# First 256 tokens' queries and keys by f32 loads of SyncE and ScalarE with a cast on chip, in a fused attention and gated FFN kernel

## The chip, the cores and the metric

The kernel runs on one core of a Trainium2 chip. Its engines each work through a list of instructions of their own, in order: TensorE (PE: matrix products and transposes; PEld is its loading of weights), VectorE (DVE), ScalarE (ACT), GpSimd (POOL) and SyncE (SP). SyncE, ScalarE and GpSimd issue the DMAs, GpSimd those that change the type on the way. An instruction can wait on semaphores; everything behind it on its engine then waits too. The metric is the device time of one execution in microseconds (us), lower is better.

## The reference

```python
# q, k, v: (4, 8, 768, 64) f32; heads 0, 2, 6 are "retrieval" heads; n_sink 4, window 64
scores = q @ k.T / sqrt(64)
causal = rel >= 0                                   # rel = query position - key position
stream_keep = causal & (is_sink | (rel < window))
mask = causal for retrieval heads, stream_keep for the other five
a = softmax(where(mask, scores, -1e9)); attn = a @ v
x = attn, heads side by side                        # (3072, 512)
g, val = x @ w_gate, x @ w_val                      # (512, 1536) each
ffn_out = (gelu(g) * val) @ w_out                   # (1536, 512)
out = x + sigmoid(x @ w_res) * ffn_out              # f32
```

## The kernel before

All products are in f16 with f32 sums. The 3072 tokens go in six chunks of 512 (`CHUNKS`); chunk 0 is the first 512 tokens of batch 0, chunk 1 takes the last 256 of batch 0 and the first 256 of batch 1, and so on. Heads go in pairs (`PAIRS`: (0,2), (4,6), (1,3), (5,7)). For a chunk, attention makes the scores of a pair (`scores`, key on the partition), their exponentials on ScalarE, masks on DVE (`ea`, `eb`, `es` are these tiles; `ek` is for the four sink keys), the sums with the values (`weigh`; `va`, `vs`, `vk` are the values as loaded, shifted by some rows, and of the sinks), a normalization into `xtok` (f32) and `x` (f16), and the features-by-tokens form `xT`, by transposes on TensorE or, for the fourth pair of chunks 3, 4 and 5, by a transposing DMA of SyncE (`to_features_dma`, `xT<-x`). Then come the gate and value products (`xT,wg` and `xT,wv`), GELU and product (`hT`), the output products (`wo,hT`), the residual gate (`wr,xT`), and the products of a scheme in the manner of Strassen (`hS`, `wS`, `wt`). Chunk 0's attention runs in two halves of 256 tokens.

Queries and keys have to stand features-by-tokens (`qT`, `kT`). For chunks 0 and 1 `loads_rows` does it: GpSimd loads rows with a cast from f32 to f16 into a staging buffer (`qks`), TensorE transposes (`L682`, tile `ps`), and DVE or ScalarE evacuates (`L693`). In chunk 0 the first 256 tokens (y=0) come in four loads of four heads, k and q in turn, the next 256 (y=1) in two loads of eight heads. Later chunks use transposing DMAs of SyncE (`loads_natural`). `load_weights` and `values` make the loads of the weights and of v, on GpSimd.

Every piece of work is a task of a graph, numbered as it is built. Nothing decides the order at build time: two tables written out in the file do. `PLAN` is the list of the task numbers in the order of emission, a letter behind a number chooses the engine of a task that several can do (a ACT, d DVE, g and p POOL, s SP), and `w39` puts in 39 filler matmuls on the tile `blank`. `PLACES` gives the slot of each buffer. Each engine gets its tasks in the order of `PLAN`; waits follow from dependences and buffers. The fillers' results are not used:

```python
    for _ in range(180):
        warm = Buf(P_ps, "warm")
        G.add("pe", 0.11, lambda e, warm=warm: e.matmul(at(warm)[:, 0:256], lhsT=blank[:, 0:128], rhs=blank[:, :], start=True, stop=True),
              [t_blank], 1e9, bufs=[warm], name="warm")
```

Of the kernel before, what the change touches and what calls it, by code (L numbers as in the profile page):

```python
# [4 lines left out]
NHEAD = 8  # L5
# [425 lines left out]
def build_kernel(nc, q, k, v, w_gate, w_val, w_out, w_res, out):  # L431
# [153 lines left out]
    def values(b, a, z, base, each, on_engines=False):  # L585
# [43 lines left out]
        for lo in cuts:  # L629
            hi = lo + 1 if each else z  # L630
            ts = []
            for dst, src, off in ((0, 64, 1), (64, 0, 0)):
# [4 lines left out]
                ts[-1].late = 2.5  # L637
            for i in range(lo, hi):
                BB.vstok[i] = ts

    def loads_rows(c, si, b, a, z):

        BB = batch(b)
# [867 lines left out]
```

## Time and profile before

| | |
|---|---|
| runs | 265.31, 265.75, 266.03 us; median 265.75 |
| span of the profiled execution | 264.3 us; with the 1.45 us that the median has beside it, 265.75 |
| TensorE busy | 254.5 us (96%), 77 of 3421 matmuls are fillers |
| DVE, ScalarE, GpSimd busy | 210.8, 155.3, 106.8 us |
| first transposes of q and k | 8.16 us |
| first scores | 11.05 us |
| first gate or value product | 22.26 us |

A span is one execution on the profiler's clock. A row of the timeline gives start, duration, engine, line, operation, output tile and inputs; a row of a stretch gives the busy time of each engine in it. The chain of work that ended last is followed back from the last instruction, each step to what released it. A DMA's landing is counted from its issue.

### The profile page before, as it was taken

What the parts mean: (1) busy time and instruction counts of PE and PEld (TensorE: products, weight loads), DVE (VectorE), ACT (ScalarE), POOL (GpSimd) and SP (SyncE); (2) the same over time, 40 slices, a digit from 0 to 9 for tenths busy, and PEclk for the clock granted to TensorE, in tenths of its full rate; (3) what the DMA queues carried; (4) which work ended last, traced back from release to release, by engine and by line L of the source; (5) the groups of instructions that cost most, each with busy time, mean ns of one, the idle gap of its engine ahead of it and who ended that gap; (6) DMA issues with size and microseconds to landing.
All of it is one profiled execution on the core that took longest, in us unless ns stands there. A gap on an engine that the chain in (4) does not pass through costs nothing.

```text
span 264.3 us, 8077 instructions
## 1 busy us (share of the span) xinstructions
PE 254.5 (96%) x3421; PEld 180.7 (68%) x3421; DVE 210.8 (80%) x473; ACT 155.3 (59%) x274; POOL 106.8 (40%) x145
## 2 busy tenths in 40 slices
PE   8999999999999999999998899999999998999993
PEld 5657655558567578667677477579588677778891
DVE  1499555999988978678999677999687976877985
ACT  1277534964554998564883356884655995445511
POOL 8996741990000998013976620711500111110021
PEclk9999999999999999999999999999999999999998
DMA  7999999999297999968999994899589509050004
GB/s 69 166 139 178 207 196 191 188 158 115 82 271 99 141 123 135 182 154 182 136 97 124 152 138 93 200 123 104 69 92 237 101 2 122 7 77 2 2 2 159
DMA packets 102067, 33.17 MB, mean 125 GB/s; under 512 B 88720, under 2 KB 97168, under 8 KB 102032
## 3 DMA queue, kind: packets, MB, share of 16 engines
q0 software_dynamic: 74704, 18.88, 77.3%
q1 hardware_dynamic: 26896, 13.26, 25.0%
q8 instruction: 27, 0.44, 0.7%
q10 hardware_dynamic: 432, 0.52, 0.5%
q14 instruction: 8, 0.07, 0.1%
HBM read 29.36 MB, written 10.49 MB: 151 GB/s over the span
## 4 chain that ended last, share of the span: by engine, by line
PE 87%; DVE 8%; DMA 3%; issue 1%; ACT 0%; DVEq 0%
PE ps L477 45%; PE ps L478 30%; PE ps L850 4%; PE ps L1414 4%; DMA xT<-x 3%; PE ps L682 2%; PE ps L974 2%; PE ps L1063 1%; DVE xtok L1041 1%; DVE x L1039 1%; DVE vk L598 1%; PE ps L941 1%; DVE hS L1251 0%; DVE hT L1228 0%; DVE vs L617 0%
## 5 line engine op out<-in xcount | busy, mean ns | idle before, releaser
L539 POOL DMA_DIRECT2D qks<-in_q_dram x37 | 33.2, 983 | 48.3 <-DMA qT<-qks 26.1
L1359 POOL DMA_DIRECT2D out_dram<-otile x16 | 15.6, 975 | 76.8 <-DVE otile L1355 66.2
L477 PE MATMUL ps<-xT,wg 128*128 128x512 f16 (+1 forms) x172 | 38.7, 337 | 1.4 <-DMA xT<-x 1.0
L477 PE MATMUL ps<-xT,wv 128*128 128x512 f16 (+1 forms) x172 | 38.5, 337 | 0.0
L1129 ACT ACTIVATE gact<-ps 128x512 f16<-128x512 f32 x38 | 22.1, 596 | 27.0 <-PE ps L477 18.0
L1131 DVE SCALAR_TENSOR_TENSOR hT<-gact,ps 128x512 f16<-128x512 f16 x38 | 25.8, 683 | 13.7 <-ACT gact L1129 5.8
L539 POOL DMA_DIRECT2D qks<-in_k_dram x37 | 34.8, 977 | 1.4 <-POOLq L1493 0.8
L1203 DVE TENSOR_TENSOR ps<-ps,otile 128x256 f32<-128x256 f32 x60 | 24.0, 428 | 7.7 <-PE ps L477 3.7
L1221 ACT ACTIVATE gact<-ps 128x512 f16<-128x512 f32 x30 | 16.6, 596 | 15.7 <-PE ps L477 10.8
L539 POOL DMA_DIRECT2D va<-in_v_dram x24 | 23.7, 1017 | 3.8 <-DVE va L534 3.8
L477 PEld LDWEIGHTS ps<-xT,wg 128*128 128x128 f16 x172 | 16.2, 98 | 13.1 <-DMA xT<-x 1.5
L477 PEld LDWEIGHTS ps<-xT,wv 128*128 128x128 f16 x172 | 16.6, 98 | 11.4 <-issue 0.2
L866 ACT ACTIVATE ea<-ps 128x1024 f16<-128x1024 f32 (+2 forms) x24 | 22.0, 925 | 1.4 <-PE ps L850 1.3
L1228 DVE SCALAR_TENSOR_TENSOR hT<-gact,ps 128x512 f16<-128x512 f16 x30 | 19.3, 682 | 2.6 <-PE ps L478 1.2
L1299 ACT ACTIVATE srs<-ps 128x512 f32<-128x512 f32 x22 | 13.1, 599 | 12.2 <-PE ps L478 7.8
L477 PE MATMUL ps<-wo,hT 128*128 128x256 f16 (+1 forms) x114 | 18.3, 296 | 0.0
L478 PE MATMUL ps<-xT,wg 128*64 128x512 f16 (+1 forms) x144 | 17.6, 344 | 0.0
L478 PE MATMUL ps<-xT,wv 128*64 128x512 f16 (+1 forms) x144 | 17.6, 344 | 0.0
L1041 DVE TENSOR_TENSOR xtok<-ps,rcp 128x512 f32<-128x512 f32 (+1 forms) x28 | 16.8, 608 | 0.6
L1331 DVE TENSOR_TENSOR otile<-otile,ps 128x256 f32<-128x256 f32 x33 | 13.1, 412 | 3.7 <-PE ps L477 2.4
L850 PE MATMUL ps<-qT,kT 64*128 64x64 f16 (+4 forms) x391 | 15.9, 213 | 0.1
L478 PE MATMUL ps<-wo,hT 128*64 128x256 f16 x216 | 15.6, 273 | 0.4 <-DVE otile L1325 0.4
(175 smaller groups left out, 590.4 us busy)
## 6 DMA issues: line engine op xcount, KB each, us to landing
out_dram<-xtok SPq DMA_DIRECT2D x4, 1024.0 KB, 4.8
out_dram<-otile POOLq DMA_DIRECT2D x16, 256.0 KB, 4.5
va<-in_v_dram POOLq DMA_DIRECT2D x24, 128.0 KB, 5.6
qks<-in_k_dram POOLq DMA_DIRECT2D x32, 64.0 KB, 4.9
qks<-in_q_dram POOLq DMA_DIRECT2D x32, 64.0 KB, 5.0
wv<-in_moe_w_val_dram POOLq DMA_DIRECT2D x3, 512.0 KB, 13.2
wg<-in_moe_w_gate_dram POOLq DMA_DIRECT2D x3, 512.0 KB, 11.4
wo<-in_moe_w_out_dram POOLq DMA_DIRECT2D x4, 384.0 KB, 20.9
```

The costliest lines, as they stand in the source:

```text
L477: return e.matmul(o, lhsT=lhsT, rhs=rhs, **k)
L478: return [e.matmul(o[h:h + 64], lhsT=lhsT[:, h:h + 64], rhs=rhs, **k) for h in (0, 64)][-1]
L539: return G.add(eng, issue, lambda e: e.dma_start(out_ap(), in_ap), deps, prio, bufs=bufs, dma=cost, name=name, grp=grp)
L850: return [e.matmul(at(scr)[:, oo:oo + w], lhsT=side(BB, qb, low, 1)[half, k0:k0 + 128], rhs=side(BB, qb, low, 0)[half, qq:qq + w], start=T ...
L866: return e.activation(out=o, in_=i_, func=AF.Exp, scale=SM_SCALE)
L1041: t2 = G.add("dve", c_dve(2 * n * 64), lambda e: e.tensor_tensor(out=xview(), in0=avv(0, DHEAD), in1=scale(), op=ALU.mult), [t1] + xdeps, ...
L1129: ta = G.add("act", c_act(512), (lambda gb=gb, ga=ga, gw=gw: lambda e: e.activation(out=at(ga)[:, :], in_=at(gb)[:, gw], func=AF.Gelu))(), ...
L1131: th = G.add("dve", c_dve(512), (lambda vb=vb, ga=ga, f=f, vw=vw: lambda e: e.scalar_tensor_tensor(out=hv(f), in0=at(ga)[:, :], scalar=0.5 ...
L1203: return G.add("dve", c_dve(256), lambda e: e.tensor_tensor(out=at(ps)[:, o], in0=at(ps)[:, BL], in1=at(es)[:, 0:256], op=ALU.add), deps, ...
L1221: ta = G.add("act", c_act(512), (lambda x=x, ga=ga, both=both: lambda e: e.activation(out=two(at(ga)[:, :]), in_=both(x), func=AF.Gelu))() ...
L1228: th = G.add("dve", c_dve(512), (lambda x=x, f=f, ga=ga, both=both: lambda e: e.scalar_tensor_tensor(out=two(hv(f)), in0=two(at(ga)[:, :]) ...
L1359: t = G.add("pool", 1.0, (lambda ot=ot, r0=r0: lambda e: e.dma_start(out[r0:r0 + 128, :], at(ot)[:, :], accum_op=ALU.add))(), ends + [stor ...
```

## The change

A new function `loads_first` takes the queries and keys of tokens 0 to 255 of batch 0. It makes eight loads in f32, one for each pair of heads and each of k and q (128 KB each): k on SyncE, q on ScalarE. Each goes into a part of a staging buffer that is read as f32, is cast to f16 into one of the buffers that otherwise hold `x` (a task `c16`, on DVE, ScalarE or GpSimd), is transposed on TensorE (`L667`, two pairs of heads at a time) and evacuated (`L677`). `loads_rows` now makes only y=1 in chunk 0, k and q in one staging buffer. In the last chunk, the transposing DMAs of q and k of a token tile are one group (`grp`). `PLAN` and `PLACES` are new throughout: 35 fillers instead of 77, the first run of them 11 instead of 39; some copies go from DVE to ScalarE.

```diff
 PLAN = (
-    "1 0 14 214 16 210 211 212 215 2 5 w39 240 213 241d w2 228 216 229a w4 230 236 231d 217 237d w6 411 3 6 232 412 4 233d "
+    "0 222 220 224 218 214 212 5 216 1 225 223 16 17 210 2 235 3 234 6 215 236 217g 221a w11 232 233 219a 230 231 w3 431 "
...
+    def loads_first(b, a):
+        BB = batch(b)
+        lo = a * 128
+        qb, qo = qplace[b, a]
+        tok = {}
+        st, half = [Buf(P_st), Buf(P_st)], [Buf(P_x16), Buf(P_x16)]
+        view = lambda j, p: at(st[j])[:, :].bitcast(FP32)[:, p * 256:(p + 1) * 256]
+        h16 = lambda j, p: at(half[j]).rearrange("p c i k -> p (c i k)")[:, p * 256:(p + 1) * 256]
+        for p in ORDER:
+            h = PAIRS[p][0]
+            for j, src, eng in ((1, k, "sp"), (0, q, "act")):
+                ld = G.add(eng, 0.6, (lambda src=src, j=j, p=p, h=h: lambda e: e.dma_start(
+                    view(j, p).rearrange("p (x w) -> p x w", x=2),
+                    src[b, h:h + 3:2, lo:lo + 256, :].rearrange("x (p i) d -> p x (i d)", i=2)))(),
+                    [], -60, bufs=[st[j]], dma=0.5, name="ldf")
...
+                tok[j, p] = G.flex({e: (0.4, cast(e)) for e in ("dve", "act", "pool")}, [ld], -205, bufs=[st[j], half[j]], name="c16")
+        for k_ in (0, 2):
+            ps_ = sorted(ORDER[k_:k_ + 2])
+            for j in (1, 0):
+                scr = Buf(P_ps, "scr0")
+                to, o0 = (BB.kt, lo) if j else (qb, qo)
+                tt = G.add("pe", 0.3, (lambda scr=scr, j=j, ps_=ps_: lambda e: [
+                    e.transpose(out=at16(scr)[64 * x:64 * x + 64, (m * 2 + i) * 128:(m * 2 + i + 1) * 128],
+                                in_=h16(j, p)[:, x * 128 + i * 64:x * 128 + i * 64 + 64], identity=ident[:, :])
+                    for m, p in enumerate(ps_) for i in range(2) for x in range(2)])(),
+                    [t_ident] + [tok[j, p] for p in ps_], 40 * k_ - 205, bufs=[half[j], scr], name="qkT")
...
     def loads_rows(c, si, b, a, z):
-        st = [Buf(P_st), Buf(P_st)] if c == 0 else [Buf(P_st)] * 2
+        st = Buf(P_st)
...
-        for y in range((z - a) // 2):
+        first = 0 if c else 1
+        for y in range(first, (z - a) // 2):
             lo = (a + 2 * y) * 128
-            for gi, (h0, h1) in enumerate(((0, 4), (4, 8)) if c == 0 and y == 0 else ((0, 8),)):
-                for j, src in ((1, k), (0, q)):
...
+            if c == 0:
+                loads_first(b, a)
             (loads_rows if c < ROWS_UNTIL else loads_natural)(c, si, b, a, z)
```

Three places in the engines' lists. In the rows, `[waits ...]` are semaphores: `cnt_` of an engine's progress, `dma_` of one DMA; `x7` is a run of seven equal instructions. First, TensorE from its first instruction on; before:

```order
L1414 MATMUL ps<-blank 128x256 [waits cnt_dve]
L1414 MATMUL ps<-blank 128x256 x38
L682 MATMUL ps<-ident,qks 64x128 [waits cnt_pool,dma_214]
L682 MATMUL ps<-ident,qks 64x128 x7
L1414 MATMUL ps<-blank 128x256 x2
L682 MATMUL ps<-ident,qks 64x128 [waits dma_210]
L682 MATMUL ps<-ident,qks 64x128 x7
L1414 MATMUL ps<-blank 128x256 x4
```

and after:

```order
L1457 MATMUL ps<-blank 128x256 [waits cnt_dve]
L1457 MATMUL ps<-blank 128x256 x10
L667 MATMUL ps<-ident,x 64x128 [waits cnt_dve,cnt_act,cnt_pool]
L667 MATMUL ps<-ident,x 64x128 x7
L667 MATMUL ps<-ident,x 64x128 [waits cnt_dve,cnt_act]
L667 MATMUL ps<-ident,x 64x128 x7
L1457 MATMUL ps<-blank 128x256 x3
L893 MATMUL ps<-qT,kT 128x64 [waits cnt_dve]
```

The first transposes (of q, tile `x` holds the casted rows) now wait for DVE's and ScalarE's casts and GpSimd's identity instead of a DMA, and the first scores (`L893`, formerly `L850`) stand behind 16 transposes and 14 fillers instead of 32 and 51.

Second, ScalarE and DVE at the start. ScalarE before:

```order
L693 ACT_TABLE_LOAD
L693 ACTIVATE kT<-ps 128x2x256 [waits cnt_pe]
L866 ACTIVATE es<-ps 128x512 [waits cnt_pe]
L866 ACTIVATE ea<-ps 128x768 [waits cnt_pe]
L693 ACTIVATE qT<-ps 128x2x256 [waits cnt_pe]
```

and after:

```order
L652 DMA qks<-in_q_dram 128x2x128 x4
L658 ACT_TABLE_LOAD
L658 ACTIVATE x<-qks 128x256 [waits dma_220]
L658 ACTIVATE x<-qks 128x256 [waits dma_218]
L909 ACTIVATE es<-ps 128x512 [waits cnt_pe]
```

The four loads of q are issued ahead of the table load, and two casts (of q and of k of heads 1 and 3) come before the first exponential. DVE before:

```order
L532 MEMSET vk 128x520 [waits cnt_dve]
L534 MEMSET va 128x48
L693 COPY kT<-ps 128x2x256 [waits cnt_pe]
L693 COPY qT<-ps 128x2x256 [waits cnt_pe]
L693 COPY kT<-ps 128x2x256 [waits cnt_pe] x2
L693 COPY qT<-ps 128x2x256 [waits cnt_pe] x2
L902 TENSOR_TENSOR ea<-ea,m_causal 128x2x256 [waits cnt_pool,cnt_act]
```

and after:

```order
L659 CAST x<-qks 128x256 [waits dma_224]
L659 CAST x<-qks 128x256 [waits dma_222]
L534 MEMSET va 128x48 [waits cnt_dve]
L659 CAST x<-qks 128x256 [waits dma_214]
L677 COPY qT<-ps 128x2x256 [waits cnt_pe]
L677 COPY kT<-ps 128x2x256 [waits cnt_pe]
L659 CAST x<-qks 128x256 [waits dma_210]
L532 MEMSET vk 128x520
L659 CAST x<-qks 128x256 [waits dma_212]
L677 COPY qT<-ps 128x2x256 [waits cnt_pe]
L677 COPY kT<-ps 128x2x256
L532 MEMSET vk 128x520
```

Three casts stand ahead of DVE's first evacuation, two casts and both memsets of `vk` among and behind the evacuations of the first 256 tokens.

Third, TensorE in chunk 4, up to the first product that waits for the transposing DMA of the fourth pair; before (the DMA is `dma_1419`):

```order
L478 MATMUL ps<-vk,ek 64x65 x12
L478 MATMUL ps<-wt,hT 64x256 [waits cnt_dve]
L478 MATMUL ps<-wt,hT 64x256 x5
L478 MATMUL ps<-wo,hT 64x256 [waits cnt_dve]
L478 MATMUL ps<-wo,hT 64x256 x11
L478 MATMUL ps<-wt,hT 64x256 x6
L1063 MATMUL ps<-ident,x 64x128 [waits cnt_dve,cnt_act]
L1063 MATMUL ps<-ident,x 64x128 x15
L478 MATMUL ps<-wr,xT 64x512 [waits cnt_dve]
L478 MATMUL ps<-wr,xT 64x512 x7
L478 MATMUL ps<-xT,wv 64x512 [waits cnt_dve,cnt_act]
L478 MATMUL ps<-xT,wv 64x512 x7
```

(next comes the wait for `dma_1419`), and after, in two pieces that follow each other (the DMA is `dma_1431`):

```order
L478 MATMUL ps<-vk,ek 64x65 x6
L478 MATMUL ps<-wt,hS 64x256 x2
L478 MATMUL ps<-wt,wS 64x256 x4
L1106 MATMUL ps<-ident,x 64x128 [waits cnt_dve,cnt_act]
L1106 MATMUL ps<-ident,x 64x128 x15
L478 MATMUL ps<-wo,hS 64x256 [waits cnt_act]
L478 MATMUL ps<-wo,hS 64x256 x5
L478 MATMUL ps<-wo,hT 64x256 [waits cnt_act]
L478 MATMUL ps<-wo,hT 64x256 x11
```

```order
L478 MATMUL ps<-xT,wv 64x512 [waits cnt_act,cnt_dve]
L478 MATMUL ps<-xT,wv 64x512 x3
L478 MATMUL ps<-xT,wg 64x512 [waits cnt_dve]
L478 MATMUL ps<-xT,wg 64x512 x7
L478 MATMUL ps<-wo,hS 64x256 x2
L478 MATMUL ps<-wo,wS 64x256 x4
L478 MATMUL ps<-xT,wv 64x512 [waits cnt_dve]
L478 MATMUL ps<-xT,wv 64x512 x3
L478 MATMUL ps<-xT,wg 64x512 x4
L478 MATMUL ps<-xT,wg 64x512 [waits dma_1431]
```

The piece before has in front of it, further up, 56 sums with values (`va,ea`) and others between the sums of the fourth pair (12 `vk,ek`) and the wait; after the change no sum with `va,ea` is left between the last `vk,ek` and the wait: what stands there is what the two pieces show.

More of the change, by code (lines that the diff above doesn't have):

```diff
@@ L639, in values, with cast, ev, fn @@
                 BB.vstok[i] = ts
+    def loads_first(b, a):
[13 more added lines that the diff above has]
+                    [], -60, bufs=[st[j]], dma=0.5, name="ldf")
+                def cast(on, j=j, p=p):
+                    return lambda e: (e.activation(out=h16(j, p), in_=view(j, p), func=AF.Copy) if on == "act" else
+                                      e.tensor_copy(out=h16(j, p), in_=view(j, p)))
+                tok[j, p] = G.flex({e: (0.4, cast(e)) for e in ("dve", "act", "pool")}, [ld], -205, bufs=[st[j], half[j]], name="c16")
[9 more added lines that the diff above has]
+                    [t_ident] + [tok[j, p] for p in ps_], 40 * k_ - 205, bufs=[half[j], scr], name="qkT")
+                tt.mode = "col"
+                def ev(on, scr=scr, to=to, o0=o0, ps_=ps_):
+                    def fn(e):
+                        o = at(to)[:, ps_[0]:ps_[1] + 1:ps_[1] - ps_[0], o0:o0 + 256].rearrange("c m (p i) -> c m p i", i=2)
+                        i_ = at16(scr)[:, 0:512].rearrange("c (m i p) -> c m p i", m=2, i=2)
+                        return e.tensor_copy(out=o, in_=i_) if on == "dve" else e.activation(out=o, in_=i_, func=AF.Copy)
+                    return fn
+                t = G.flex({"dve": (c_dve(512), ev("dve")), "act": (c_act(512), ev("act"))}, [tt], 40 * k_ - 205,
+                           bufs=[scr, to], name="qkE")
+                for p in ps_:
+                    for i in range(a, a + 2):
+                        (BB.ktok if j else BB.qtok)[p, i] = t
@@ L647, in loads_rows, with sv, piece @@
         tok = {}
-        def sv(j, h0, h1, y):
-            if c == 0:
-                return at(st[j])[:, :].rearrange("p (h w) -> p h w", h=NHEAD)[:, h0:h1, y * 128:y * 128 + 128]
-            return at(st[j])[:, :].rearrange("p (j h w) -> p j h w", j=2, h=NHEAD)[:, j, h0:h1, :]
-        def piece(j, h, i, y):
-            o = h * 256 + y * 128 if c == 0 else (j * NHEAD + h) * 128
-            return at(st[j])[:, o + i * 64:o + (i + 1) * 64]
-        for y in range((z - a) // 2):
-            lo = (a + 2 * y) * 128
-            for gi, (h0, h1) in enumerate(((0, 4), (4, 8)) if c == 0 and y == 0 else ((0, 8),)):
-                for j, src in ((1, k), (0, q)):
-                    t = dma("pool", base + 4 * gi + 8 * y + 1 - j, (h1 - h0) * n * (0.092 if c else 0.089),
-                            (lambda j=j, h0=h0, h1=h1, y=y: lambda: sv(j, h0, h1, y))(),
-                            src[b, h0:h1, lo:lo + 256, :].rearrange("h (p j) d -> p h (j d)", j=n), bufs=[st[j]])
-                    t.late = 1.0 if c else 0.7
-                    for h in range(h0, h1):
-                        tok[j, h, y] = t
+        def sv(j):
+            return at(st)[:, :].rearrange("p (j h w) -> p j h w", j=2, h=NHEAD)[:, j]
+        def piece(j, h, i):
+            o = (j * NHEAD + h) * 128
+            return at(st)[:, o + i * 64:o + (i + 1) * 64]
+        first = 0 if c else 1
+        assert (z - a) // 2 - first == 1
+        for y in range(first, (z - a) // 2):
+            lo = (a + 2 * y) * 128
+            for j, src in ((1, k), (0, q)):
+                t = dma("pool", base + 8 * y + 1 - j, NHEAD * n * 0.092, (lambda j=j: lambda: sv(j))(),
+                        src[b, :, lo:lo + 256, :].rearrange("h (p j) d -> p h (j d)", j=n), bufs=[st])
+                t.late = 1.0
+                for h in range(NHEAD):
+                    tok[j, h, y] = t
         values(b, a, z, base + (10 if c == 0 else 2), False, c == 0)
         per = 2 if c == 0 else 4
-        for y in range((z - a) // 2):
+        for y in range(first, (z - a) // 2):
             lo = (a + 2 * y) * 128
@@ L679, in loads_rows, with tr @@
                     to = BB.kt if js[0] else qb
-                    def tr(e, items=items, scr=scr, y=y):
+                    def tr(e, items=items, scr=scr):
                         return [e.transpose(out=at16(scr)[64 * x:64 * x + 64, (m * n + i) * 128:(m * n + i + 1) * 128],
-                                            in_=piece(jj, h, i, y), identity=ident[:, :])
+                                            in_=piece(jj, h, i), identity=ident[:, :])
                                 for m, (p, jj) in enumerate(items) for i in range(n) for x, h in enumerate(PAIRS[p])]
                     tt = G.add("pe", c_mm(128, n) * len(items), tr, [t_ident] + [tok[jj, h, y] for p, jj in items for h in PAIRS[p]],
-                               pr, bufs=[st[js[0]], scr], name="qkT")
+                               pr, bufs=[st, scr], name="qkT")
                     tt.mode = "col"
@@ L726, in loads_natural @@
                 t = G.add("sp", 1.65, (lambda sv=sv, to=to, o0=o0: lambda e: e.dma_start(
-                    at(to)[:, :, o0:o0 + 128], sv(), transpose=True))(), ds, base, bufs=[st, to], dma=0.85, name="dT")
+                    at(to)[:, :, o0:o0 + 128], sv(), transpose=True))(), ds, base, bufs=[st, to], dma=0.85, name="dT",
+                          grp=("dT", b, i) if c == len(CHUNKS) - 1 else None)
                 t.late = 2.5
```

152 rows, old and new, of tables (PLACES, PLAN) are left out of this document.

## The prediction

> **What bounds the kernel now.** I read the page first: the busy times, the slices, the chain of work that ended last.
>
> ```profile
> span 264.3 us, 8077 instructions
> ...
> PE 254.5 (96%) x3421; PEld 180.7 (68%) x3421; DVE 210.8 (80%) x473; ACT 155.3 (59%) x274; POOL 106.8 (40%) x145
> ...
> PEclk9999999999999999999999999999999999999998
> ...
> PE 87%; DVE 8%; DMA 3%; issue 1%; ACT 0%; DVEq 0%
> ```
>
> TensorE is busy for 96% of the span and carries 87% of the chain. Some of that busy time is filler matmuls on a blank tile, so the question is in which stage TensorE is busy with nothing. Next came the table of stretches: start to first transposes, from there to the first gate/value matmul, the dense part after it (each row: stretch, length, busy time of PE, PEld, DVE, ACT, POOL with counts, granted clock, DMA share, GB/s).
>
> ```profile
> 0.00:8.16 8.16, 6.95 (x39) 5.08 (x40) 0.84 (x4) 1.28 (x1) 6.97 (x14) 1.00 0.93 87
> 8.16:22.26 14.10, 13.78 (x240) 8.99 (x240) 11.54 (x31) 8.68 (x19) 13.65 (x25) 1.00 1.54 152
> 22.26:139.00 116.74, 116.36 (x1268) 77.17 (x1268) 96.50 (x216) 76.99 (x131) 58.17 (x75) 1.00 1.37 158
> ```
>
> Until 8.16 us nothing useful runs on TensorE: its 39 matmuls are fillers. In the next 14.10 us DVE works 11.54 and 38 of TensorE's 240 matmuls are fillers. From 22.26 us on TensorE idles 0.38 us in 116.74: it is the bound there, so an earlier first gate/value matmul is worth its whole amount if nothing later takes it back. The timeline and the chain of the start say what holds that matmul (timeline: start, duration, engine, line, tile, count, idle before).
>
> ```profile
> 0.82 1.28 ACT L693 ACT_TABLE_LOAD   x1 [0.82 <-PEq L1493]
> ...
> 1.21 7.03 PE L1414 MATMUL ps<-blank 128*128 128x256 f16 x39 [1.21 <-DVE blank L511]
> ...
> 3.21 0.77 POOL L539 DMA_DIRECT2D qks<-in_q_dram  x1
> ...
> 8.16 0.41 PE L682 MATMUL ps<-ident,qks 128*64 128x128 f16 x8
> ...
> 8.62 0.69 DVE L693 COPY kT<-ps 128x512 f16<-128x512 f16 x1 [6.58 <-PE ps L682]
> ...
> 10.17 0.69 DVE L693 COPY qT<-ps 128x512 f16<-128x512 f16 x1 [0.87 <-PE ps L682]
> ...
> 11.72 0.69 DVE L693 COPY kT<-ps 128x512 f16<-128x512 f16 x1 [0.27 <-PE ps L682]
> ...
> 12.89 1.47 DVE L693 COPY qT<-ps 128x512 f16<-128x512 f16 x2 [0.47 <-PE ps L682]
> ...
> 22.26 1.03 PE L477 MATMUL ps<-xT,wv 128*128 128x256 f16 x8
> ```
>
> ```profile
> 14.28 0.41 DVE ea L902
> ...
> 23.10 0.44 DVE xtok L1041
> ```
>
> GpSimd issues the q load at 3.21 and TensorE's transposes follow at 8.16, 4.9 us later. From the first mask at 14.28 to a normalization at 23.10 the chain stands on DVE; before that DVE waits, up to 0.87 us, for TensorE's transposes, which wait for landings. So loads hold the first half of the stage, DVE the second.
>
> **The change, part by part.** Prices come from these rows: small hardware-queue DMAs, casts of twice the width, the `vk` memset, and last the landing of GpSimd's q and k loads in the first 8 us.
>
> ```profile
> L1371 SPq DMA_DIRECT2D out_dram<-otile x5: 332/578/1313, 72.7 to 260.3; - x5
> L1371 ACTq DMA_DIRECT2D out_dram<-otile x3: 338/338/375, 257.5 to 261.6; - x3
> ...
> DMA to landing us min/median/max: 1.7/2.0/3.7
> ```
>
> ```profile
> L1048 DVE CAST x<-xtok x2: 428/532/635, 141.8 to 219.9; 128x512 f16<-128x512 f32 x2
> ```
>
> ```profile
> L1047 ACT ACTIVATE x<-xtok x8: 621/629/632, 63.0 to 223.1; 128x512 f16<-128x512 f32 x8
> ```
>
> ```profile
> L532 DVE MEMSET vk<- x2: 492/492/492, 1.3 to 36.4; 128x520 f16 x2
> ```
>
> ```profile
> DMA to landing us min/median/max: 4.1/4.9/5.7
> ```
>
> (1) *The first transposes.* They need the identity, the first two q loads, a cast of one on ScalarE and of the other on DVE; the k pair behind them needs ScalarE's second cast. ScalarE starts at 0.82 and issues four loads (0.338 each by its own row, 0.578 by SyncE's: to 2.2 or 3.1), then the table load (1.28), which now stands behind the issues (to 3.5 or 4.4), then a cast of 256 elements, half the width of the row with 0.629, so 0.3 to 0.6: between 3.8 and 5.0, and I take the middle, 4.4. Landings are not the later branch by the nearest rows: stores of the same queues land in 1.7 to 2.0 us, so loads issued by 1.5 are there by 3.5. If they took what GpSimd's q took, 4.9, the transposes would start at 1.5 + 4.9 + 0.4 = 6.8. I take the stores, since the queue is the same: 8.16 − 4.4 = **−3.8 us** (from −4.4 to −1.4). Nothing hides it: eleven fillers end about 3.5 and TensorE then waits.
>
> (2) *DVE's new work.* DVE does five of the eight casts; three stand before its first evacuations, where it was idle, two among the evacuations: 2 × 0.27 to 0.43 (half the row's median up to its minimum), 0.7. One `vk` memset of 0.49 ran at 1.3 us in idle time, the other at 36.4; now both stand between evacuations: 1.0. **+1.7 us** (0.7 if waits for TensorE cover the memsets, 1.9 at most). Waiting behind them are the evacuations of the second pairs, then masks and ScalarE's exponentials.
>
> (3) *Idle on DVE closed.* From 8.62 to 14.28 before, DVE idled 0.87 + 0.27 + 0.47 = 1.6 us for transposes (the brackets of the timeline's rows). The y=1 loads are now issued second and third by GpSimd instead of after four others, so half of it should go: **−0.8** (0 to −1.6). The first gate/value matmul then stands at 22.26 − 3.8 + 1.7 − 0.8 = 19.4.
>
> (4) *GpSimd and the weights.* Four loads leave GpSimd's queue (4 × 0.8), one cast enters and waits for its landing, holding the later v and weight loads. The first gate weights move ahead of the first value weights. Weights have to be there at 19.4 and not 22.26: the first value and gate loads took
>
> ```profile
> DMA to landing us min/median/max: 5.9/13.2/16.8
> ...
> DMA to landing us min/median/max: 7.5/11.4/15.0
> ```
>
> (value, then gate). With gate issued near 9.9 and value near 13.9 (0.77 us an issue, by the q row, and about 0.5 a mask, copy or memset ahead of them), they land at 9.9 + 7.5 = 17.4 and 13.9 + 5.9 = 19.8. I cost it at 0; without that cover the value products wait up to about 0.5.
>
> (5) *Order of the rest.* Copies move from DVE to ScalarE (80% against 59% busy): 0, hidden behind TensorE. What can show is the feature DMA of chunks 3 to 5, `xT<-x` (its landing over all three; then chunk 4's alone; then the chain at chunk 3's and the timeline at chunk 4's).
>
> ```profile
> DMA to landing us min/median/max: 3.7/4.9/7.4
> ```
>
> ```profile
> L1054 SPq DMA_TRANSPOSE xT<-x x1: 1232/1232/1232, 180.8 to 180.8; - x1
> ...
> DMA to landing us min/median/max: 4.9/4.9/4.9
> ```
>
> ```profile
> 142.46 7.36 DMA xT<-x
> ...
> 149.86 2.33 PE ps L477 x10
> ```
>
> ```profile
> 179.30 0.38 PE L478 MATMUL ps<-vk,ek 128*64 128x65 f16 x12
> ...
> 183.80 0.82 PE L478 MATMUL ps<-wo,hT 128*64 128x256 f16 x12
> 184.45 0.50 PE L478 MATMUL ps<-wt,hT 128*64 128x256 f16 x6
> 184.78 0.62 PE L1063 MATMUL ps<-ident,x 128*64 128x128 f16 x16
> 185.23 1.03 PE L478 MATMUL ps<-wr,xT 128*64 128x512 f16 x8
> 186.09 1.47 PE L478 MATMUL ps<-xT,wv 128*64 128x512 f16 x12
> ```
>
> From starts, a 256-column half matmul costs 0.65/12 = 54 ns, a 512-column one 0.86/8 = 107 ns, 16 transposes 0.45. Chunk 4 before: the last sums of its fourth pair end at 179.68, the DMA is issued at 180.8 and lands at 185.7, 6.0 us after; 56 attention matmuls and others fill that time. After: from the last `vk,ek` to the waiting row stand 30 of 54 ns, 16 transposes and 20 of 107 ns: 1.6 + 0.45 + 2.1 = 4.2 us, short by 1.8; if the earlier `vk,ek` were the pair's last, it is 5.8, short by 0.2. I take **+1.0** (0.2 to 3.2, the last by the longest landing, 7.4). Chunk 3, where 7.36 us ended late, has 27 × 0.109 + 8 × 0.215 + 0.3 = 5.0 us of cover (whole columns cost double) against 4.7: **−0.3** (−1.7 if it lands as chunk 5's did, 0 at worst). Chunk 5 keeps 5.4 against 1.2 + 3.7: 0.
>
> Sum: −3.8 + 1.7 − 0.8 + 0 + 1.0 − 0.3 = −2.2. The profiled execution took 264.3 plus 1.45 around it, 265.75, the runs' median: **263.5 us**.
>
> **The rivals.** *Half clock (slower).* The fillers show two rates, though the granted clock reads 1.00 in both stretches (columns as above, PE and PEld alone).
>
> ```profile
> 1.21:6.54 5.33, 5.33 (x26) 3.80 (x27) 1.00 0.91 84
> 6.54:8.07 1.53, 1.53 (x15) 1.27 (x13) 1.00 1.70 161
> ```
>
> 205 ns each for 5.3 us of unbroken work, 102 ns after it. Eleven fillers end after 2.3 us, TensorE pauses, and sparse transposes follow, so the fast rate may come late. Price: the stage's matmuls that are not fillers take about 13.78 − 38 × 0.109 = 9.6 us at the fast rate and 19 at the slow one, against 15 us from 4.4 to 19.4: +4 when slow all through; with 5.3 us of dense gate work at half speed, another 2.65. If it ends in between, one of the two, or about 1. It decides above 3.1 us (263.5 to 266.6): both in part, +4, is **267.5**. For it: fillers fall from 77 to 35. Against: slow matmuls fill TensorE, and full work raised the rate in the trace. The Trainium skill, "TensorE: Matmul & The Clock Gate", Part 1, says the array runs at half rate until one busy window of about 3.4 us and that the window runs freely; this trace's 5.3 us agrees with a window that began 1.9 us into the fillers, and by the rule the slow rate would go on until such a window is full, which is this rival.
>
> *Loads no quicker (same).* The loads land as GpSimd's did, 4.9 us: the transposes come at 6.8, the term is −1.4, the sum +0.2: **265.9**. For it: eight loads, 1 MB, run beside GpSimd's own. Against: store rows of 2.0. The Trainium skill, "DMA: Bandwidth & Descriptors", "Issuing engines are not separate DMA queues", says these queues end on the same 16 engines as GpSimd's; then only issue time is saved. No row here shows a load on these two queues; by that rule alone the time would be this rival's.
>
> *The whole shift.* DVE's extra work hides in its idle time and chunk 4 does not stall: −3.8 − 0.8 + 0.7 − 0.3 = −4.2: **261.5**. DVE at 11.54 of 14.10 speaks against it.
>
> *The start does nothing:* a gain of 2.9 is made and chunk 4's stall and the weights give back 3.2 + 0.5: **266.3**; it needs the longest landing.
>
> **How the numbers follow.** Forecast 0.48 (262.2 to 264.8, from terms 1 and 5), whole shift 0.15, loads no quicker 0.12, stall gives all back 0.05, half clock above 3.1 us 0.20. 0.3% (0.8 us) is about what a measurement of this kernel can tell from no change: faster means under 264.95. Faster takes 0.48 + 0.15 and a small part of the loads' case, 0.65; the same 0.15; slower 0.20. The range leaves a tenth on either side: 260.8 (whole shift with term 1 and chunk 3 at their better ends) to 267.5.
>
> **What the profile after would show.** First transposes at 3.8 to 5.0, first gate/value matmul at 19.0 to 20.0 (term 3 wrong if DVE still idles between evacuations), DVE on the chain from there back to about 8 us. `xT<-x` on the waits of TensorE for 0.5 to 1.5 us near chunk 4. Loads landing after 4.5 make term 1 wrong; filler spacings of 205 ns after 10 us, or gate matmuls twice as long, make the half clock the cause.

## The result: slower by 5%, and the profile after

The changed kernel takes 279.1 us (median of 4 runs, 277.31 to 280.77) against 265.53 before (4 runs, 264.97 to 266.03): a ratio of 1.0498, 95% interval 1.0431 to 1.0564. The forecast was 263.5. The profiled execution took 277.63 us. Medians here hold all runs; ratios leave out those that fell in a slower state of the chip, which any kernel can meet.

The page of the changed kernel, in the lines that answer to those of before:

```profile
span 275.4 us, 8022 instructions
...
PE 254.3 (92%) x3395; PEld 177.0 (64%) x3395; DVE 205.3 (75%) x462; ACT 162.2 (59%) x292; POOL 104.6 (38%) x142
...
PEclk9999999999999999999999689999999999999998
...
PE 65%; DMA 19%; POOL 7%; DVE 4%; issue 2%; ACT 1%; ACTq 1%; SPq 0%; DVEq 0%
```

TensorE's busy time is as before (254.5), though it has 42 fillers less to do; the span grew by 11.1. Transfers (DMA), 3% of the chain before, carry 19%. One slice of the clock row drops to 6. To see where the time went, I took from both traces the moment at which TensorE had done equal amounts of work that is not filler (in us at full rate):

| work done | before | after | difference |
|---|---|---|---|
| 1 | 11.12 | 9.34 | −1.8 |
| 7 | 22.78 | 22.79 | 0.0 |
| 43 | 60.33 | 60.28 | 0.0 |
| 49 | 67.00 | 68.49 | +1.5 |
| 97 | 115.95 | 117.18 | +1.2 |
| 103 | 122.06 | 124.53 | +2.5 |
| 127 | 147.33 | 149.34 | +2.0 |
| 133 | 154.64 | 164.63 | +10.0 |
| 229 | 253.78 | 264.27 | +10.5 |

So the start gains 1.8 us and has lost it by 23 us; 1.5 go at 61 us and 1.2 at 119; 8 go at 150. TensorE's waits name the last three (us in total, times, longest):

```profile
PE ps L477 <- DMA xT<-x: 7.3, 1, 7.3
PE ps L1017 <- DMA vs<-va: 1.6, 1, 1.6
...
PE ps L477 <- DVE ps L1246: 0.8, 1, 0.8
PE ps L478 <- DMA xT<-x: 0.5, 1, 0.5
```

**150 us, chunk 3.** The chain before and then after, to the transposing DMA of chunk 3's fourth pair:

```profile
137.96 1.03 PE ps L477 x22
```

```profile
145.30 0.70 DVE xtok L1084
...
146.02 0.81 DVE x L1091
...
146.85 10.33 DMA xT<-x
```

TensorE's timeline after, around the wait:

```profile
144.59 0.26 PE L477 MATMUL ps<-vk,ek 128*128 128x65 f16 x3
...
149.15 0.82 PE L477 MATMUL ps<-wo,hT 128*128 128x256 f16 x6
...
157.23 1.04 PE L477 MATMUL ps<-xT,wg 128*128 128x512 f16 x2 [7.26 <-DMA xT<-x]
158.06 1.06 PE L477 MATMUL ps<-xT,wv 128*128 128x512 f16 x2
...
161.93 1.02 PE L477 MATMUL ps<-xT,wg 128*128 128x512 f16 x4
162.79 0.60 PE L477 MATMUL ps<-xT,wv 128*128 128x512 f16 x2
```

The row of the same wait in the kernel before:

```profile
149.86 0.61 PE L477 MATMUL ps<-xT,wg 128*128 128x512 f16 x2 [1.05 <-DMA xT<-x]
```

Before, the pair's last sums ended at 138.99 and the transfer landed 10.9 us later; the product that waits was reached 9.8 us after them, hence 1.05 of wait. After, the last sums end at 144.85, the landing comes 12.4 us later, and TensorE's other work lasts 5.1 us beyond the sums (to 149.97). Cover nearly halved and a landing of 10.3 instead of 7.4 make 7.26 us of wait. Then two 512-column products take 0.83 us (157.23 to 158.06) where four take 0.86 later (161.93 to 162.79): half rate, for some 3.6 us, with 1.8 us lost. 7.3 − 1.05 + 1.8 is the step of 8.0 in the table. The stretch of 15 us, after and then before (busy times in the order PE, PEld, DVE, ACT, POOL, then the granted clock):

```profile
150.00:165.00 15.00, 7.77 (x35) 3.89 (x36) 4.36 (x10) 3.15 (x7) 0.14 (x1) 0.77 1.16 116
```

```profile
150.00:165.00 15.00, 15.00 (x106) 10.21 (x105) 11.74 (x28) 8.22 (x20) 3.51 (x5) 1.00 1.06 130
```

The DMA column is alike (1.16 and 1.06), so it is one transfer that is late, not the engines that stand still. GpSimd's timeline shows what is just ahead of it: 15 loads and stores that start between 136.3 and 146.3 us, after 5.8 us without any. Before, it was eight, from 136.8 to 141.8 us, ahead of a transfer issued at 142.46.

**The start.** TensorE after:

```profile
5.10 1.07 PE L667 MATMUL ps<-ident,x 128*64 128x128 f16 x16 [1.45 <-DVE x L659]
...
7.91 0.39 PE L893 MATMUL ps<-qT,kT 64*128 64x64 f16 x8 [0.98 <-DVE kT L677]
...
10.14 1.46 PE L1457 MATMUL ps<-blank 128*128 128x256 f16 x6
...
16.00 0.50 PE L1457 MATMUL ps<-blank 128*128 128x256 f16 x3
...
22.48 0.60 PE L477 MATMUL ps<-xT,wg 128*128 128x256 f16 x4
```

Transposes come 3.1 us earlier, scores too (7.91 against 11.05), the first gate product does not (22.26 before). Six fillers take 1.46 us at 10.14: half rate, nine us after the first matmul. The page's issues (tile, queue, count, KB each, median us to landing) show the new loads beside stores of the same size on the same queue:

```profile
qks<-in_q_dram ACTq DMA_DIRECT2D x4, 128.0 KB, 4.2
qks<-in_k_dram SPq DMA_DIRECT2D x4, 128.0 KB, 3.7
...
out_dram<-otile ACTq DMA_DIRECT2D x4, 128.0 KB, 1.8
```

The chain through the start and on to 61 us:

```profile
2.39 5.60 DMA qks<-in_q_dram
...
8.06 0.94 POOL x L659
...
9.95 2.65 POOL va L539 x3
...
28.60 24.75 DMA va<-in_v_dram
...
54.12 7.45 DMA vs<-va
```

GpSimd's cast waits for the last q load until 8.06, and three v loads stand behind it. The v load issued at 28.60, behind four output weights of 384 KB, lands after 24.75 us; the wait at 61 hangs on it. Of the step at 119 us: TensorE waits for an addition of DVE (`ps L1246`), which waits for two things that end together here, a store that GpSimd issues at 112.03 us (landed at 119.02) and a copy of ScalarE (119.06).

### The profile page after: what moved, and what is told of

It is laid out like the page before. It is cut to its first block, busy times and chain, and to the rows that moved or that the text cites. A ratio compares the mean times of both kernels' runs of the same rounds, so it can differ in the third digit from the quotient of the medians.

```text
span 275.4 us, 8022 instructions
## 1 busy us (share of the span) xinstructions
PE 254.3 (92%) x3395; PEld 177.0 (64%) x3395; DVE 205.3 (75%) x462; ACT 162.2 (59%) x292; POOL 104.6 (38%) x142
## 4 chain that ended last, share of the span: by engine, by line
PE 65%; DMA 19%; POOL 7%; DVE 4%; issue 2%; ACT 1%; ACTq 1%; SPq 0%; DVEq 0%
PE ps L477 30%; PE ps L478 29%; DMA va<-in_v_dram 9%; DMA xT<-x 5%; PE ps L893 3%; DMA vs<-va 3%; DMA qks<-in_q_dram 2%; POOL va L539 2%; POOL qks L539 2%; PE ps L1017 1%; POOL wo L539 1%; PE ps L1106 1%; POOL wv L539 1%; DVE xtok L1084 1%; DVE otile L1398 1%
## 5 line engine op out<-in xcount | busy, mean ns | idle before, releaser
L1402 POOL DMA_DIRECT2D out_dram<-otile x16 | 16.2, 1075 | 83.9 <-DVE otile L1398 83.9
L477 PE MATMUL ps<-xT,wg 128*128 128x512 f16 (+1 forms) x172 | 40.1, 342 | 7.4 <-DMA xT<-x 7.3
L1172 ACT ACTIVATE gact<-ps 128x512 f16<-128x512 f32 x38 | 21.9, 597 | 39.7 <-PE ps L477 20.6
L539 POOL DMA_DIRECT2D qks<-in_q_dram x35 | 30.5, 966 | 29.1 <-DMA qT<-qks 13.3
L477 PE MATMUL ps<-xT,wv 128*128 128x512 f16 (+1 forms) x168 | 39.2, 345 | 0.0
L539 POOL DMA_DIRECT2D qks<-in_k_dram x35 | 32.3, 943 | 17.4 <-PE ps L724 10.2
L1246 DVE TENSOR_TENSOR ps<-ps,otile 128x256 f32<-128x256 f32 x60 | 24.3, 428 | 8.3 <-PE ps L478 3.6
L539 POOL DMA_DIRECT2D va<-in_v_dram x24 | 25.1, 1094 | 9.2 <-PE ps L1017 7.9
L909 ACT ACTIVATE ea<-ps 128x1024 f16<-128x1024 f32 (+2 forms) x24 | 21.4, 928 | 2.0 <-PE ps L893 1.9
L1271 DVE SCALAR_TENSOR_TENSOR hT<-gact,ps 128x512 f16<-128x512 f16 x30 | 19.6, 683 | 1.0 <-PE ps L477 0.8
L1374 DVE TENSOR_TENSOR otile<-otile,ps 128x256 f32<-128x256 f32 x33 | 13.6, 417 | 8.5 <-PE ps L478 6.9
L478 PE MATMUL ps<-xT,wv 128*64 128x512 f16 (+1 forms) x152 | 18.7, 341 | 0.0
L893 PE MATMUL ps<-qT,kT 64*128 64x64 f16 (+4 forms) x391 | 17.0, 218 | 1.3 <-DVE kT L677 1.0
L1242 ACT ACTIVATE ps<-ps 128x256 f32<-128x256 f32 x25 | 9.3, 371 | 12.4 <-PE ps L477 9.1
```

Source lines behind the costliest of these rows:

```text
L477: return e.matmul(o, lhsT=lhsT, rhs=rhs, **k)
L478: return [e.matmul(o[h:h + 64], lhsT=lhsT[:, h:h + 64], rhs=rhs, **k) for h in (0, 64)][-1]
L539: return G.add(eng, issue, lambda e: e.dma_start(out_ap(), in_ap), deps, prio, bufs=bufs, dma=cost, name=name, grp=grp)
L893: return [e.matmul(at(scr)[:, oo:oo + w], lhsT=side(BB, qb, low, 1)[half, k0:k0 + 128], rhs=side(BB, qb, low, 0)[half, qq:qq + w], start=T ...
L909: return e.activation(out=o, in_=i_, func=AF.Exp, scale=SM_SCALE)
L1172: ta = G.add("act", c_act(512), (lambda gb=gb, ga=ga, gw=gw: lambda e: e.activation(out=at(ga)[:, :], in_=at(gb)[:, gw], func=AF.Gelu))(), ...
```

## The experiments

Two theories. A: the new order costs the time, above all chunk 3's late transfer (A1: because GpSimd's burst is ahead of it in the DMA engines). B: the new loads set everything behind them back. For the start there are C, the half rate, and D, the landings of v. Times are medians beside kernel-before runs on the same chip, and ratios carry their 95% interval.

**Loads and order taken apart.** Two kernels that join one order to the other, each with renumbered tasks.

```diff
 # newloads_oldorder: PLAN is the first 144 entries of the order after,
+# then all the rest in the order of before
 # oldloads_neworder: loads_rows for y=0 as before; the first 120 entries of the order before,
+# then all the rest in the order after
```

> The new loads and casts, and the first 144 entries of the new order (to the end of chunk 0's scores), then everything in the order of before. Theory A (the order costs the time, above all the wait for xT<-x in chunk 3; the new start gains 1.8 us at the first scores and has lost it by 22.8 us): 264 to 267 us, no wait over 2 us for xT<-x. Theory B (the eight loads and casts themselves put the stream of loads behind and every later stage with it): 271 us or more.

> The loads of before, and the first 120 entries of its order, then everything in the new order. Theory A: 275 to 280 us, with a wait of 5 to 8 us for xT<-x in chunk 3. Theory B: 268 us or less and no such wait.

The first took 278.71 us against 266.15 (1.0461, 1.0392 to 1.0529), the second 283.79 (1.0682, 1.0624 to 1.0740). Theory A's numbers came in neither: 264 to 267 and 275 to 280 us were expected, and of the second a wait of 5 to 8 us, where 4.5 was measured. B's for the second (268 us or less, no such wait) failed as well. Both totals hold long waits at the place where the orders meet. Waits of TensorE, new loads with the old order:

```profile
PE ps L724 <- DMA qks<-in_q_dram: 4.6, 1, 4.6
PE ps L477 <- DMA wv<-in_moe_w_val_dram: 3.9, 1, 3.9
```

and old loads with the new order:

```profile
PE ps L682 <- DMA qks<-in_k_dram: 7.6, 1, 7.6
PE ps L477 <- DMA xT<-x: 4.5, 1, 4.5
```

The 3.9 and 4.6 lie at 22 and 30 us, the 7.6 at 24: weights and loads of one order come late for the other's products. So neither total decides between the theories. What does count: the long wait for `xT<-x` appears with the old loads under the new order, and is absent with the new loads under the old. By equal work the second kernel loses 6.3 us at chunk 3, the changed kernel 8.0, the first nothing.

```diff
 # newloads_oldorder2: PLAN as in newloads_oldorder (144 entries of after, then the order of before),
+# except 13 entries: GpSimd's loads of v and of the weights stand in the order of before
```

> As newloads_oldorder, but GpSimd's loads of v and the weights stand in the order of before (the first version loaded gate weights first and then began with the value product, a wait of 8.5 us that the mixing made). New loads and casts, the new order up to chunk 0's scores, then the order of before. Theory A (order, not loads): 263.5 to 267 us, no wait over 1.5 us after 25 us. Theory B (the new loads themselves set the whole stream back): 270 or more.

272.49 against 265.63 (1.0239, 1.0179 to 1.0300): this is where B put it (270 or more), and A's other sign failed too, since there are waits of 1.4 us at 95 and 2.5 at 208 to 211. Its waits:

```profile
PE ps L1106 <- DVE x L1082: 2.6, 2, 1.9
PE ps L984 <- DMA qT<-qks: 2.5, 1, 2.5
...
PE ps L893 <- DMA q<-kT: 1.4, 1, 1.4
```

The first gate product came 2.7 us later than before, behind a wait of 1.9 us for DVE; half rate follows that wait (21.8 to 24.5 us) and the one of 2.5 (212.5 to 215.7). Chunk 3 has no wait for `xT<-x`, which landed in 4.9 us. So the new loads cost something under this order, and B is not refuted by this run: whether the loads themselves do it, or this order, which was not written for them, is not shown. What speaks against B as the main cause are the edits that follow: they keep all eight new loads in the order of after and bring the time back (`va_v`).

**Chunk 3, with the order of after.** Six loads are held until the last cast ahead of the transfer. The store of the expectation is not held; it goes ahead of them, at 142.42 us instead of 145.72:

```diff
-    (in PLAN) 394 ... 415 ... 391 ... 409 ... 412 ... 1126 ... 397
+    (in PLAN) 1126 394 415 391 409 412 397    # behind 1195
+    for n in (394, 415, 391, 409, 412, 397):
+        G.tasks[n].deps.append(G.tasks[1188])
```

> The changed kernel, but six loads of later chunks (and one store) that GpSimd issues in the 5 us ahead of chunk 3's xT<-x wait for the cast that releases xT<-x. Theory A1 (the transposing DMA lands late because it stands behind those transfers): landing 10.3 falls to 6 us or less, TensorE's wait from 7.3 to under 3, time 269.5 to 273. Theory A2 (the cast is late, the landing would be as long without them): landing 9 us or more, time 276 to 280.

The four runs took 269.56, 269.70 (the profiled one), 275.46 and 277.54 us (median 272.58, against 266.15). They lie too far apart for a ratio, and the two long ones have no trace; what decides is the landing. The chain and the wait of the profiled run:

```profile
146.19 5.63 DMA xT<-x
```

```profile
PE ps L477 <- DMA xT<-x: 2.5, 1, 2.5
```

The same transfer at the same place lands in 5.6 us instead of 10.3 when six of GpSimd's loads are not ahead of it. That shows A1. There is no half rate after this shorter wait. Then the transfer itself was taken away:

```diff
-                if c > DT_FIRST and P.p == order[1]:
+                if c > 3 and P.p == order[1]:
     (in PLAN) the transposes and evacuations of chunk 3's fourth pair, ahead of its first value product
```

> The changed kernel with the fourth pair of chunk 3 transposed on TensorE (16 transposes' worth of columns and two evacuations) instead of by the DMA. Theory A: the wait of 7.3 us goes and so do some 1.8 us of half clock behind it, at a price of under 1.5 us: 268 to 271. Rival (the products wait as long for something else, the evacuations or the pair's normalization): 274 or more.

269.69 against 266.15 (1.0134, 1.0079 to 1.0190): 9.4 us below after, as A said; neither the wait nor the half rate is left at 150 us. What stays are these:

```profile
PE ps L1017 <- DMA vs<-va: 1.1, 1, 1.1
...
PE ps L477 <- DVE ps L1246: 0.7, 1, 0.7
```

**The v loads of chunk 1.** On top of `c3_petranspose`, three v loads go ahead of the output weights:

```diff
-    (in PLAN) 528 206 207 ... 554 259 258 533 556 578 269
+    (in PLAN) 528 259 258 269 206 207 ... 554 533 556 578
```

> c3_petranspose with three v loads of chunk 1 issued ahead of the four loads of the output weights instead of behind them. Theory A (the wait of 1.1 us at 61 us is the order of these loads in one stream): that wait goes, the time is 0.6 to 1.5 us less. Rival: the output weights come late instead, a new wait of 0.5 us or more near 45 to 55 us and no gain.

267.77 us (11 runs) against 265.63 (1.0065, 1.0035 to 1.0095); the wait for `vs<-va` is gone and no new one takes its place, which by equal work is worth 1.1 us. The ratios so far are 1.0498, 1.0134 and 1.0065; the intervals of the last two overlap, so the gain of this step rests on the trace. At the start this trace has a spell of half rate (19.6 to about 23 us, after a wait of 0.6), which `c3_petranspose` with the same fillers did not have.

**The half rate at the start.** On top of `c3_petranspose`, more fillers:

```diff
-    "... 236 217g 221a w11 232 233 219a 230 231 w3 431 ..."
+    "... 236 217g 221a w19 232 233 219a 230 231 w8 431 ..."
```

> c3_petranspose with 19 fillers instead of 11 ahead of the first transposes and 8 instead of 3 behind them, all in time in which TensorE waited. Theory C (the slow rate until 14 us holds the first stage): the rate rises before 9 us, the first gate product comes 0.7 us or more earlier than in c3_petranspose, the time is 0.5 to 1.5 us less than its. Rival D (DVE and landings hold that stage): the rate rises but the first gate product moves by less than 0.3 us, the time is the same within 0.5.

272.27 against 265.63 (1.0245, 1.0194 to 1.0296): 2.6 us more, where C had less and D the same. TensorE's timeline:

```profile
14.53 0.45 PE L477 MATMUL ps<-va,ea 128*128 128x65 f16 x5 [1.38 <-DMA va<-in_v_dram]
...
20.03 1.04 PE L1457 MATMUL ps<-blank 128*128 128x256 f16 x4
...
21.71 1.49 PE L1457 MATMUL ps<-blank 128*128 128x256 f16 x6
...
24.37 0.60 PE L477 MATMUL ps<-xT,wg 128*128 128x256 f16 x4
```

The full rate came at 3.8 us, scores and transposes ran faster, TensorE reached the first value sums early and waited 1.4 us for v. From the end of that wait to 24.2 us the rate is half (sums stand 54 ns apart instead of 29), and the first gate product came at 24.37, 2.5 us later than in `c3_petranspose` (21.83). More is lost at 119 us: TensorE waits 3.2 us for DVE's addition there (`ps L1246`), with half rate from 123.2 to 126.6; by equal work this kernel is 1.6 us behind the kernel before up to there and 6.7 after.

With the v loads of `f3_va` as well:

> Both edits on c3_petranspose. If both theories hold, the gains add: 1.1 to 3.0 us less than c3_petranspose, 266.5 to 268.5. If the first stage is held by DVE, only that of the v loads.

268.84 (10 runs; 1.0115, 1.0073 to 1.0157), no better than `f3_va` and above the 266.5 to 268.5 expected: the v loads moved so far are chunk 1's, and the wait at 14 us (1.3 us here) is for chunk 0's. So, on top of `f3_va`, GpSimd's cast goes to ScalarE, and three v loads move up:

```diff
-    "... 215 236 217g 221a w11 232 233 219a 230 ... 8 237 426 238 ... 251 239 423 ..."
+    "... 215 236 237 238 221a w11 232 233 219a 217a 230 ... 239 8 426 ... 251 423 ..."
```

> f3_va with GpSimd's one cast moved to ScalarE and two of the four v loads of chunk 0 issued right behind the first (in the changed kernel they stood behind that cast, which waits for a q load until 8 us; f3_warm showed TensorE waiting 1.4 us for v at 13 to 14.5 us). Theory E (GpSimd's queue, held by the cast, sets the first stage): second and third v land 1 to 3 us earlier, the gate weights too, the first gate product is 0.5 us or more earlier than in f3_va. Rival (the slow rate of TensorE sets it as long as fillers are few): the loads land earlier, the first gate product moves by under 0.3 us, time within 0.5 of f3_va's 267.8.

266.80 (11 runs) against 265.69: 1.0011 (0.9976 to 1.0047). As theory E said, the loads come earlier: second and third v at 12.19 and 13.09 us instead of 13.25 and 16.79, gate weights at 17.0 instead of 20.6. The first gate product stands at 21.85 instead of `f3_va`'s 23.61, but that one came behind its spell of half rate, and `c3_petranspose` had it at 21.83 without these loads, so it is not shown that they moved it. The time is 1.0 us below `f3_va`'s, with intervals that overlap. Still, with chunk 3's transfer replaced, v loads moved and all eight new loads kept, no difference from the kernel before can be told. With `w19` and `w8` on top:

> va_v with 19 and 8 fillers as in f3_warm. If slow rate and v loads hold the stage in turn, neither helps alone and both together do: no wait for v at 13 to 14.5 us, no second spell of slow rate from 16 to 22 us, the first gate product at 20.5 us or before, time 264.5 to 266.5. If the slow spell comes back although the wait for v is gone: 267 to 270.

267.02 (11 runs), 1.0070 (1.0035 to 1.0106). The mechanism is there: TensorE at full rate from 3.9 us with no relapse, no wait for v, and the first gate product 1.35 us earlier than before. The numbers missed: 20.91 where 20.5 or less was expected, and a time above 264.5 to 266.5, with a ratio no better than `va_v`'s:

```profile
10.00 0.83 PE L1457 MATMUL ps<-blank 128*128 128x256 f16 x6
...
20.91 0.60 PE L477 MATMUL ps<-xT,wg 128*128 128x256 f16 x4
```

By equal work it is 1.6 us ahead from 23 us and 2.0 at 114, then 0.3 behind at 122. Its chain, and TensorE's wait there:

```profile
108.91 7.92 DMA out_dram<-otile
```

```profile
PE ps L477 <- DVE ps L1246: 1.8, 1, 1.8
```

A 256 KB store, issued in a row of GpSimd's loads, frees its tile late; TensorE comes earlier, the store does not. It was moved nine entries up:

```diff
-    (in PLAN) 897a 885 942 ... 903 888 982
+    (in PLAN) 897a 885 888 942 ... 903 982
```

> va_v_warm with one 256 KB store of the output (the one whose buffer DVE waits for near 118 us, TensorE behind it) issued nine entries earlier on GpSimd's queue, ahead of three v loads. The wait of 0.5 to 3 us near 119 us goes: 0.5 to 1.5 us less than va_v_warm, 264 to 266. Rival: the time is the same, since the next store or DVE's own work ends last there.

268.65 (11 runs), 1.0056 (1.0012 to 1.0100): that wait goes, and waits of 1.2 and 1.8 us for later transfers of SyncE (`q<-qT` at 131, `vs<-va` at 138 us) come in its place. The time is that of the rival, the reason is not: it named the next store or DVE's own work.

**The fillers of before.** Last, the kernel before with the first run of fillers as short as after's:

```diff
-    "1 0 14 214 16 210 211 212 215 2 5 w39 240 213 241d w2 ..."
+    "1 0 14 214 16 210 211 212 215 2 5 w11 240 213 241d w2 ..."
```

> The kernel before with 11 fillers instead of 39 at the start and nothing else: TensorE idles from about 3.5 us to its first transposes at 8.2. Theory C (unbroken work raises the rate, thin work does not): the slow rate lasts until 11 us or later, the first gate product stands 0.5 to 3 us later than 22.3, the time is 266.3 to 269. Rival (the slow rate costs nothing there, since landings and DVE hold that stage): first gate product within 0.3 us of 22.3, time the same within 0.5 us.

268.24 against 265.86 (12 runs; 1.0061, 1.0025 to 1.0097), as C said. Its fillers are still slow at the place where after's are, and in its first pause TensorE waits for the identity:

```profile
9.77 1.46 PE L1414 MATMUL ps<-blank 128*128 128x256 f16 x6
```

```profile
PE ps L682 <- POOL ident L497: 2.4, 1, 2.4
```

Half rate lasts to 12.5 us instead of 6.5, the first gate product comes at 22.97 instead of 22.26, and the trace shows further waits of 1 to 2 us for transfers later on. One thing more stands in this trace: its first transposes come at 6.14 us, 2.0 earlier than before, though the k load they need lands at 5.9 us in both. So in the kernel before it is the 39 fillers, and not the loads, that hold the first transposes until 8.16; the scores, which need q as well, come at 11.17 and 11.05. The 28 fillers cost 2 us at the first transposes, and with them the full rate came 6 us earlier.

None of these kernels beats the one before.

## Why the prediction was wrong, step by step

**Term 5, chunk 3, is the step that failed**: "5.0 us of cover against 4.7", −0.3. The 5.0 for after was right (5.1 measured). The 4.7 for before was not: it counted the work from a late `vk,ek` row in the order, while the chain shows that the sums which feed the transfer had ended at 138.99, 9.8 us ahead of the wait. So cover was halved where I had it growing. The landing was taken at its value of before, 7.4, and was 10.3, since GpSimd's burst now stands ahead of it: what GpSimd issues ahead of the transfer has no place in the term. Cost: 8.0 instead of −0.3. That alone turns 263.5 into 271.8.

**Chunk 4**, +1.0 (0.2 to 3.2): 0.54 measured. The cover came as counted (4.3 us against 4.2), by the method that chunk 3 was not given: the sums of the pair were looked up in the trace. The size is partly luck: the transfer landed in 3.7 us, where 4.9 was put in, and with 4.9 the wait would have been some 1.7.

**Term 1**, −3.8 (−4.4 to −1.4): −3.1. "Landings are not the later branch" was wrong: the first pairs landed in 2.7 to 3.3 us and the medians were 3.7 and 4.2, which lies nearer to the 4.9 of the rival "loads no quicker" than to the 2.0 of the stores, taken as the nearest rows. The second q load took 4.64, and its cast brings the start of the transposes to 5.10. Besides, the term counts from 8.16 as if loads held the transposes there; `before_w11` shows that some 2.0 of the 3.1 us come with fewer fillers alone.

**Terms 2 and 3**, +1.7 and −0.8, first gate product at 19.4: it came at 22.48. DVE's casts and memsets cost what was said (0.22 to 0.33 and 0.49 each). Its idle was not closed: it waits 1.07 us for transposes that stand behind GpSimd's cast (8.06 to 9.00, a cast to which the prediction gave no price), and 0.99 for transposes at half rate (16 of them 1.07 to 1.16 us instead of 0.64). The half rate is the rival half clock: real, to 14 us here, and with the wait in chunk 3 once more, but not the main cause. Its size at the start: `va_v_warm` brings the product forward by 0.94 us against `va_v` and 0.92 against `c3_petranspose`. What fills the time from there to 19.4 no run shows.

**Term 4**, 0: the weights were in time for 22.48, but not as worked out: the gate weights were issued at 13.03 instead of 9.9 and landed at 20.90 instead of 17.4, and at 19.4 they would have held the product. The v loads of chunk 0 behind the cast cost nothing in after; `f3_warm`, at full rate earlier, waits 1.4 us for them. All later loads were put at nothing without a reason; chunk 1's v load costs 1.5 us, and the step at 119 us, where the store is one of two that end last, 1.2.

**The rest of the order** has in term 5 a price for the copies ("0, hidden behind TensorE") and for `xT<-x`, and none for the loads and the stores that moved. TensorE, busy for 96% of the span, had hidden them before; in after it waits where a transfer has moved behind a burst (at 150 and 61 us). The misses add up: 8.3 in chunk 3, 3.1 at the start, 1.5 at 61 us, 1.2 at 119, −0.5 in chunk 4 make 13.6, and between the span by the forecast (264.3 − 2.2 = 262.1) and the measured 275.4 lie 13.3.

The Trainium skill, "DMA: Bandwidth & Descriptors", "Issuing engines are not separate DMA queues", says that transfers of all issuers share the same 16 engines and interleave; `c3_hold` agrees (10.3 to 5.6 us), and it was the rule to apply to chunk 3, not just to the start. "TensorE: Matmul & The Clock Gate" of the same skill, Part 1, has the rate halve after an idle window of about 3.4 us: the 7.3 us wait followed by half rate, and the 2.5 us wait of `c3_hold` without it, agree. In `f3_warm` half rate followed a wait of 1.4 us, in `newloads_oldorder2` waits of 1.9 and 2.5; these are shorter than such a window, and there the measurement decides.

**Open.** The price of the new loads under an order made for them and equal otherwise was not measured, since the kernels that join the orders wait where they meet. What sets the moments at which the full rate comes and goes also stays open (next section). Giving the store at 119 us to another issuer, away from the loads, was not tried.

## What to carry to other kernels

Where a new order is written for the whole kernel, follow each wait on a transfer that the profile of before shows just hidden (here 1.05 us of wait at 150): take from the chain when its last producer ended, count what the new order leaves between that and the waiting instruction, and add the DMAs now issued ahead of it; a share of busy time says nothing on it. A landing time belongs to a backlog, not to a kind of transfer. Fillers that look like waste can matter: without 28 of them the full rate came 6 us later (`before_w11`). And a gain at the start was lost here where the transfers of later stages did not come earlier with it (119, 131 and 138 us in `va_v_warm` and `va_v_warm_out`).

## What the runs showed of the hardware that was not expected

- One kind of transfer on one queue landed in 5.6 or 10.3 us by what GpSimd had issued ahead of it; a 128 KB load in 24.75 behind 1.5 MB of weights.
- TensorE's half rate came back after a wait of 7.3 us (157.2 to 160.8), and after shorter ones: 3.2 and 1.4 us in `f3_warm` (123.2 to 126.6, 14.5 to 24.2), 2.5 and 1.9 in `newloads_oldorder2` (212.5 to 215.7, 21.8 to 24.5), 0.6 in `f3_va` (19.6 to about 23). After the 2.5 us of `c3_hold` it did not.
- The full rate came after 5.3 us of unbroken fillers in the kernel before, after 3.2 in `oldloads_neworder` with the same opening, and after 2.6 and 2.8 in `f3_warm` and `va_v_warm` (starts at 1.13 to 1.21 us). `f3_warm_va` and `va_v_warm_out` open like the last two, and their 19 fillers all ran at half rate. So it differs between executions of one opening. With 11 fillers and then a pause it came between about 12.5 and 14.2 us.
- The row of the granted clock reads full in slices at the start where fillers are 0.21 us apart; there the spacing is what to read.
